# Values kept in DRAM and loaded pair by pair, with a longer ring of weight tiles and another slot order, in a fused attention and gated-MLP kernel

## The chip, the cores and the metric

The kernel runs on one core of one Trainium2 chip. The metric is the device time of one execution in microseconds, taken as the median of three runs.

## The reference, cut to what matters

```python
xn = _layernorm(x, axis=-1)                      # x: 2048 x 512, float32
return x + _A_ref(xn, A_wqkv, A_wo) + _B_ref(xn, B_w_in, B_w_sp, B_b_sp, B_w_out)

# A: 32 heads of 16 columns
q, k, v = qkv[0], qkv[1], qkv[2]
scores = jnp.einsum("bhqd,bhkd->bhqk", q, k) * (Dh ** -0.5)
p = _softmax(scores, axis=-1)
o = jnp.einsum("bhqk,bhkd->bhqd", p, v)
return (lambda x, *d: x.transpose(*d))(o, 0, 2, 1, 3).reshape(B, S, D) @ wo

# B: F = 1792, Fh = 896
z = _gelu(jnp.einsum("bsd,df->bsf", x, w_in))
z1 = z[..., :Fh]
z2 = _layernorm(z[..., Fh:], axis=-1)
g = jnp.einsum("ts,bsf->btf", w_sp, z2) + b_sp[None, :, None]
return jnp.einsum("bsf,fd->bsd", z1 * g, w_out)
```

## The kernel before

**The attention.** The 32 heads run as 16 pairs. For one pair and 512 query columns (a quarter), 16 key tiles of 128 rows are passed. For each key tile TensorE makes the scores of both heads (`scores`, L1232, two matmuls at L1245 into one of three PSUM buffers `sl`), ScalarE takes the exponential into a tile `pf` (`exp`, L1223; `PF` = 8 such tiles), and TensorE multiplies it with V (`values`, L1336, matmuls at L1352). The result of 8 key tiles is added up by `part_out` (L1365). The whole V, with a column of ones behind the 16 columns of each head so that the row sums come out of the same matmul, stays in SBUF as one tile, `vall` (L107); `vpack` (L1010) picks the columns of one head from it, and `v_out` (L422) evicts each 128 rows of V into it with one copy.

**The maxima.** The largest score of each row is needed before the exponential. TensorE makes the scores a second time in the other orientation, one pair ahead (`maxima`, L1251, matmuls at L1259), VectorE reduces 128x1024 of them at a time (`max_red`, L840), and after each 16 such slots `max_fin` (L845 to L860) transposes the maxima, stores them in DRAM (`mscr`) and loads them back as two more rows of the stacked q (`qst`). This is called the exchange here; there are 64. The next scores need its result.

**The dense work.** Everything else that TensorE does is cut into slots of two or four matmuls that a queue of generators hands out: q, k and v, the two halves of the MLP's input product (z2, then z1), the spatial product with w_sp, its output product, and the attention's output product (`attn_out`, L931). One slot is taken by `dense_slot` (L1304, matmuls at L1310) and its results go to PSUM buffers named `dps`. Weights arrive as float32 in a raw tile and are split by POOL into a high and a low part in a second tile (`weight`, L276). Both tiles come from one ring of `RING` = 19 tiles of 128x2x512 (`piece`, L232), in which a raw tile uses one half of its room.

**The order of the work.** TensorE's order is fixed when the program is built, by a planner that keeps a clock of its own for each engine (the `while` loop under `last_turn`). It walks through two strings in turn:

```python
ORDER = ('SMDDSDDMDSDDMDDSDMDDSDMDDSDMDDSDMDDSDDMDMV', 'SMDDDDSDMDDSDMDDSDMDDSDMDDDSDMDDSDDDDMSV')
```

S is a score slot, M a maxima slot, D a dense slot, and V multiplies the 8 P tiles of the string with V. One string up to and with its V is called a cycle here; there are 137, and each holds 8 S, 9 or 7 M in turn, and 24 D. Where no dense slot is ready at the planner's clock (its weights have not been split by then, or the buffers `dps` are not free), a filler stands (`filler`, L1319, matmuls of zeros at L1324). Near the end of the program, when no maxima are left, the planner takes scores and products with V singly. The first cycles are preceded by a written-out opening (`STEPS`, class `First`), which makes the first quarter of q, k, v and the first maxima.

**The end.** The last pair's sums go through `last_pair` (L960), `last_norm` (L974, L976), `last_mm` (L984) and `last_add` (L998, L1003); the dense part of the attention output of two row tiles is added by VectorE at L935 into the tile `fin` that the last add completes. Loads and most stores are issued on SP (`move` and `later`, L142), in the order in which the planner emits them; some stores go out on POOL.

## Time and profile before

| what | value |
|---|---|
| time, median of 3 runs | 1834.79 us (1834.34 to 1835.03) |
| profiled execution, span from first to last instruction | 1830.4 us |
| TensorE (PE) busy | 1800.6 us, 98% of the span, 14742 matmuls |
| VectorE (DVE) busy | 1443.2 us, 79% |
| ScalarE (ACT) busy | 1211.4 us, 66% |
| GpSimd (POOL) busy | 684.5 us, 37% |
| mean granted TensorE clock | 0.999 of full speed |
| DMA engines, hardware queue | 53.3% of the span of 16 engines |

The span is that of one profiled execution; its own time as the runs count it is not given apart from the span, so the 4.4 us between span and median are taken together. A busy share is an average over the whole program. PE counts as busy from a matmul's start to its modelled end, so 98% says that something almost always ran there, not what it was worth.

### The profile page before, as it was taken

The numbers are of one execution on the slowest core, as the hardware profiler recorded it, in microseconds if no ns is written. First come the engines' busy times: TensorE is split into PE (matmuls) and PEld (weight loads), VectorE is DVE, ScalarE is ACT, GpSimd is POOL, SyncE is SP. The second block draws the span as 40 slices with busy tenths as digits, with TensorE's granted clock in tenths as the row PEclk, the third lists the DMA queues.
The fourth block names the chain that finished last, engine by engine and source line by source line (L and its number), as shares of the span: only waits on it lengthen the run. The fifth ranks groups of instructions, "written<-read, shape, count | busy, mean of one in ns | idle before, by whom it ended". The sixth has DMA issues, their size and how long they took to land.

```text
span 1830.4 us, 38100 instructions
## 1 busy us (share of the span) xinstructions
PE 1800.6 (98%) x14742; PEld 1087.6 (59%) x14742; DVE 1443.2 (79%) x1696; ACT 1211.4 (66%) x1329; POOL 684.5 (37%) x786
## 2 busy tenths in 40 slices
PE   9999999999999999999999999999999999999998
PEld 6666566666556565565656655656566665656543
DVE  8857787888888787787877887778778877888882
ACT  4257777888877777666666665666666665666655
POOL 5452241777767776212532244103422140002201
PEclk9999999999999999999999999999999999999999
DMA  7876654433664237647757568655757477466423
GB/s 265 280 240 227 201 190 128 123 114 114 180 190 132 95 105 209 163 137 186 227 144 204 159 188 201 166 143 158 190 146 181 141 210 170 121 156 168 136 88 104
DMA packets 214910, 305.64 MB, mean 167 GB/s; under 512 B 37744, under 2 KB 107952, under 8 KB 214720
## 3 DMA queue, kind: packets, MB, share of 16 engines
q1 hardware_dynamic: 207240, 275.93, 53.3%
q0 software_dynamic: 7488, 27.27, 4.3%
q8 instruction: 116, 1.90, 0.4%
q14 instruction: 66, 0.54, 0.1%
HBM read 193.27 MB, written 109.85 MB: 166 GB/s over the span
## 4 chain that ended last, share of the span: by engine, by line
PE 89%; DVE 5%; DMA 3%; issue 1%; SPq 1%; ACT 1%; POOL 0%; DVEq 0%; ACTq 0%; POOLq 0%
PE dps L1310 35%; PE sl L1352 24%; PE sl L1245 14%; PE sl L1259 12%; DVE mm L840 4%; PE dps L1324 1%; SPq L142 1%; DMA wsp_14r<-in_w_spT 1%; DMA zs<-z2scr 1%; DMA mscr<-ms 0%; PE sl L984 0%; DMA x<-in_x 0%; ACT pf L86 0%; DMA qst<-mscr 0%; DMA qst<-qscr 0%
## 5 line engine op out<-in xcount | busy, mean ns | idle before, releaser
L840 DVE TENSOR_REDUCE mm<-sl 128x2 f32<-128x1024 f32 x1008 | 1208.3, 1222 | 186.0 <-PE sl L1259 177.4
L86 ACT ACTIVATE pf<-sl 128x1024 f32<-128x1024 f32 x1024 | 1043.1, 1026 | 326.7 <-PE sl L1245 288.6
L1352 PE MATMUL sl<-pf,vall 128*32 128x512 f32 x4096 | 467.9, 595 | 0.6 <-DVE on L974 0.6
L1245 PE MATMUL sl<-qst,kst 50*128 50x512 f32 x2048 | 434.6, 417 | 7.7 <-DVE mm L840 2.2
L1259 PE MATMUL sl<-kst,qst 48*128 48x512 f32 x2016 | 414.9, 404 | 3.9 <-DVE mm L840 2.6
L1310 PE MATMUL dps<-wsp,zs 64*128 64x512 f32 x2352 | 381.6, 392 | 0.9 <-DMA zs<-z2scr 0.6
L1245 PEld LDWEIGHTS sl<-qst,kst 50*128 50x128 f32 x2048 | 194.4, 184 | 220.3 <-issue 81.6
L1352 PEld LDWEIGHTS sl<-pf,vall 128*32 128x32 f32 x4096 | 119.2, 109 | 266.5 <-issue 234.9
L1259 PEld LDWEIGHTS sl<-kst,qst 48*128 48x128 f32 x2016 | 191.8, 185 | 104.2 <-ACT pf L86 49.5
L1310 PEld LDWEIGHTS dps<-wsp,zs 64*128 64x128 f32 x2352 | 228.7, 187 | 36.8 <-DMA zs<-z2scr 1.2
L86 ACT ACTIVATE e<-sl 128x512 f32<-128x512 f32 x64 | 38.3, 598 | 189.9 <-PE sl L1352 177.8
L1374 DVE TENSOR_TENSOR e<-sl,e 128x512 f32<-128x512 f32 x64 | 44.2, 691 | 130.2 <-PE sl L1352 80.5
L743 POOL TENSOR_TENSOR hhl<-z1i,hhl 128x512 fp32r<-128x512 f32 x28 | 35.9, 1292 | 280.6 <-ACT hhl L86 280.6
L1310 PE MATMUL dps<-w,xt 64*128 64x448 f32 x768 | 110.5, 368 | 1.7
L1310 PE MATMUL dps<-wout,hp 64*128 64x512 f32 x672 | 110.5, 393 | 0.1
L891 POOL TENSOR_TENSOR ob<-ob 128x512 f32<-128x512 f32 (+1 forms) x16 | 20.6, 1287 | 173.0 <-DMA ob<-rscr 173.0
L1310 PEld LDWEIGHTS dps<-w,xt 64*128 64x128 f32 x768 | 73.7, 186 | 16.1 <-issue 8.4
L1310 PEld LDWEIGHTS dps<-wout,hp 64*128 64x128 f32 x672 | 64.2, 187 | 10.4 <-issue 0.6
L397 POOL TENSOR_TENSOR qkhl<-qr,qkhl 128x512 fp32r<-128x512 f32 x24 | 30.3, 1280 | 97.3 <-ACT qkhl L86 83.0
L887 POOL TENSOR_TENSOR ob<-ob 128x512 f32<-128x512 f32 (+1 forms) x16 | 20.6, 1287 | 99.3 <-DMA ob<-escr 99.3
L1310 PE MATMUL dps<-wf,zs 64*128 64x512 f32 x336 | 55.5, 392 | 0.1
L1310 PE MATMUL dps<-xnT,wqk 64*128 64x512 f32 x288 | 47.9, 394 | 0.3
(298 smaller groups left out, 1692.4 us busy)
## 6 DMA issues: line engine op xcount, KB each, us to landing
zs<-z2scr SPq DMA_DIRECT2D x192, 256.0 KB
escr<-e SPq DMA_DIRECT2D x60, 256.0 KB
hscr<-hhl POOLq DMA_DIRECT2D x28, 512.0 KB, 5.9
qst<-qscr SPq DMA_DIRECT2D x60, 192.0 KB
kst<-kscr SPq DMA_DIRECT2D x60, 192.0 KB
qscr<-qkhl SPq DMA_DIRECT2D x16, 512.0 KB
kscr<-qkhl SPq DMA_DIRECT2D x16, 512.0 KB
xt<-xscr SPq DMA_DIRECT2D x64, 128.0 KB
```

Of the source, the lines that this page charges most:

```text
L86: return nc.scalar.activation(out, in_, func, **kw)
L142: nc.sync.dma_start(raw(dst), raw(src))
L397: nc.gpsimd.tensor_sub(hl[:, 1, :], raw_, hl[:, 0, :].bitcast(F32))
L743: nc.gpsimd.tensor_sub(hl[:, 1, :], z1, hl[:, 0, :].bitcast(F32))
L840: nc.vector.tensor_reduce(mmax[g][:, :, t, kc], sl[k], AX.X, ALU.max)
L887: nc.gpsimd.tensor_add(both_[rows, 0, :], both_[rows, 0, :], both_[rows, 1, :])
L891: nc.gpsimd.tensor_mul(both_[rows, 0, :], both_[rows, 0, :], both_[rows, 1, :])
L1245: nc.tensor.matmul(sl[k][:, j, :], kst[p % 2][rows, kt * P:(kt + 1) * P], qst[p % 2][rows, c * 512:(c + 1) * 512], start=True, stop=True)
L1259: nc.tensor.matmul(sl[k][:, j, :], qst[p % 2][rows, tt * P:(tt + 1) * P], kst[p % 2][rows, kc * 512:(kc + 1) * 512], start=True, stop=True)
L1310: nc.tensor.matmul(bank_of(bank)[:, :w], lhs, rhs, start=go, stop=stop)
L1352: nc.tensor.matmul(sl[k][cols:cols + VW, 0, :], vpack(kt + r, 2 * p + j), pf[:, j * 512:(j + 1) * 512], start=n % CYC == 0, stop=n % CYC = ...
L1374: nc.vector.tensor_add(e, sl[k][:, 0, :], e)
```

## The change

V no longer stays in SBUF. Each 128 rows of V are evicted into a stage tile that is taken from the ring of P tiles (`pf`, now 10 instead of 8), with ones in every 17th column, and stored from there to a new DRAM tensor `vscr`; the 32 columns of pair 0 are also copied straight to their place. Two tiles `vpair` hold the columns of the pair in use and of the next one; `load_v` loads a pair's columns with four DMAs, queued when the pair before has passed its first 8 key tiles (40 for the first). While V is still being made, `exp` leaves two of the ten P tiles to the stages. The ring of weight tiles grows from 19 to 24 tiles, and two raw weight tiles share one tile of it, half each. Both strings of the slot order are new, with the same counts of S, M and D.

```diff
-RING = 19
+RING = 24
-ORDER = ('SMDDSDDMDSDDMDDSDMDDSDMDDSDMDDSDMDDSDDMDMV', 'SMDDDDSDMDDSDMDDSDMDDSDMDDDSDMDDSDDDDMSV')
-PF = 8
+ORDER = ('SMDDSDDMDSDDMDDSMDDDSDMDSDDMDDSDMDDSDDDMMV', 'SMDDDDSDMDSMDSDDDMDDSDMDDDSDMDDSMDDDDDSV')
+PF = 10
...
-    vall = cp.tile([P, NT * H * (DH + 1) + DH - 1], F32, name="vall")
+    vpair = [cp.tile([P, 2 * NT * (DH + 1) + DH - 1], F32, name=f"vpair{a}") for a in range(2)]
...
+    vscr = dr.tile([P, NT, H * (DH + 1)], F32, name="vscr")
...
+    def raw_half(nm):
+        if shared:
+            pair, rest = shared.pop()
+            return pair[:, 1, :], rest
+        pair, rest = piece(nm).bitcast(F32), [2]
+        shared.append((pair, rest))
+        return pair[:, 0, :], rest
...
-        rw = begin(*a)
+        rw, rest = raw_half(nm + "r")
...
-        lease("big", 1)
+        rest[0] -= 1
+        if not rest[0]:
+            lease("big", 1)
...
+    def v_stage(t):
+        vs = at_.tile([P, H * (DH + 1)], F32, tag="pf", name=f"vs{t}", bufs=PF).rearrange("p (h d) -> p h d", d=DH + 1)
+        nc.gpsimd.memset(vs[:, :, DH:], 1.0)
+        return vs
+    def v_take(t, src, copy):
+        copy(vhead(0, t), src[:, 0:2 * DH].rearrange("p (h d) -> p h d", d=DH))
+        vs = staged.pop(t)
+        copy(vs[:, :, :DH], src.rearrange("p (h d) -> p h d", d=DH))
+        return vscr[:, t, :], vs.rearrange("p h d -> p (h d)")
...
     def v_out(t, bank, k):
...
+        while not pfq:
+            yield "C", lambda: pfq
+        gps(0.4)
+        start = pfq.pop(0)
+        staged[t] = v_stage(t)
...
+        store(*pair)
+        pfq.append(ends[0] + 3.0)
...
+    def vpack(p, t, j):
+        i = (2 * t + j) * (DH + 1)
+        return vpair[p % 2][:, i:i + VW]
+    def load_v(p):
+        for i in range(4):
+            w = 2 * (DH + 1)
+            dst = vpair[p % 2][:, 4 * i * w:4 * (i + 1) * w].rearrange("p (t x) -> p t x", x=w)
+            later(0.5 * i, move, dst, vscr[:, 4 * i:4 * i + 4, w * p:w * (p + 1)])
...
-            while not pfq:
-                yield "C", lambda: pfq
+            while not pfq or len(pfq) < 3 and len(vdone) < NT - EARLY:
+                yield "C", lambda: len(pfq) > (0 if len(vdone) == NT - EARLY else 2)
...
+            if vloaded[0] <= p and p + 1 < NP and n_pv >= 64 * p + (40 if p == 0 else 8):
+                vloaded[0] = p + 1
+                load_v(p + 1)
```

TensorE, start of the 31st cycle, where z1 begins, before the change. L1352 is the product with V that closes the cycle ahead, L1245 a score slot, L1259 a maxima slot, L1324 a filler.

```order
L1352 MATMUL sl_202<-pf_5787,vall 32x512 x2
L1245 MATMUL sl_201<-qst_91,kst_93 128x512 x2
L1259 MATMUL sl_203<-kst_92,qst_90 128x512 x2
L1324 MATMUL dps<-brow,zeror 128x512 x2
L1245 MATMUL sl_202<-qst_91,kst_93 128x512 x2
L1324 MATMUL dps<-brow,zeror 128x512 x4
```

The same place in the changed program (product with V L1401, scores L1294, maxima L1308, dense slots L1359):

```order
L1401 MATMUL sl_204<-pf_5861,vpair_88 32x512 x2
L1294 MATMUL sl_203<-qst_92,kst_94 128x512 x2
L1308 MATMUL sl_205<-kst_93,qst_91 128x512 x2
L1359 MATMUL dps<-xnT_0__5734,wf_0_5500 128x512
L1359 MATMUL dps<-xnT_0__5734,wf_0_5523 128x512
...
L1294 MATMUL sl_204<-qst_92,kst_94 128x512 x2
```

Dense slots of z1 stand where the fillers stood. The listings show such fillers inside the cycles of before at the 31st, 32nd, 47th and 48th, around the 62nd, 76th, 90th and 104th and in the last ones; in the changed program every cycle from the third to the last few has its 24 dense slots but the 36th (none, and no fillers) and the 48th (12 fillers instead).

SP, the end of the opening, before: `qst` and `kst` are the stacked q and k, `xscr` the store of the normalized x, `wqk` raw weights, `mscr` the exchange of the maxima.

```order
L142 DMA kst_92<-kscr_98 48x512
L142 DMA xscr_0_102<-xnT_0_349 128x1024
L142 DMA xscr_1_103<-xnT_1_326 128x1024
L142 DMA xscr_2_104<-xnT_2_343 128x1024
L142 DMA xscr_3_105<-xnT_3_353 128x1024
L142 DMA wqk_0r<-in_wqkv 128x4x128
L142 DMA wqk_1r<-in_wqkv 128x4x128
L142 DMA wqk_0r<-in_wqkv 128x4x128
L142 DMA mscr_163<-ms_794 128x32
...
L142 DMA qst_90<-mscr_163 2x16x32 x2
```

And in the changed program:

```order
L142 DMA vscr<-vs_693 128x544
L142 DMA vscr<-vs_717 128x544
L142 DMA qst_91<-qscr_95 48x512
...
L142 DMA vscr<-vs_751 128x544
L142 DMA vscr<-vs_776 128x544
L142 DMA xscr_0_103<-xnT_0_351 128x1024
...
L142 DMA wqk_0r<-in_wqkv 128x4x128 x3
L142 DMA mscr_165<-ms_811 128x32
L142 DMA wqk_0r<-in_wqkv 128x4x128
L142 DMA qst_91<-mscr_165 2x16x32 x2
```

Four stores of V have come in, two of them ahead of the last loads of q and k and two ahead of the stores of x. Further on, the loads of `load_v` (three or four of a pair's four) stand between the store and the reload of the maxima in 15 of the 64 exchanges.

TensorE, in the last cycles, before; L1310 is a dense slot of the attention's output product.

```order
L1245 MATMUL sl_202<-qst_91,kst_93 128x512 x2
L1310 MATMUL dps<-wo_18433,op_0_19789 128x512 x2
L1245 MATMUL sl_203<-qst_91,kst_93 128x512 x2
L1310 MATMUL dps<-wo_18449,op_0_19789 128x512 x6
L1310 MATMUL dps<-wo_18463,ohl_3_19478 128x512 x2
L1245 MATMUL sl_202<-qst_91,kst_93 128x512 x2
L1352 MATMUL sl_201<-pf_19972,vall 32x512 x2
```

And in the changed program:

```order
L1294 MATMUL sl_204<-qst_92,kst_94 128x512 x2
L1373 MATMUL dps<-brow,zeror 128x512 x2
L1294 MATMUL sl_205<-qst_92,kst_94 128x512 x2
L1373 MATMUL dps<-brow,zeror 128x512 x6
L1294 MATMUL sl_204<-qst_92,kst_94 128x512 x2
L1401 MATMUL sl_203<-pf_20038,vpair_88 32x512 x2
```

The dense slots of the last rows have moved ahead of this place, and fillers (L1373) stand there.

## Rows read from the trace of the kernel before

**Rows 1.** View of the core, and part 1 of the page (busy us, share, instructions).

```profile
core 0: 1830.4 us, clock 0.999
...
PE 1800.6 (98%) x14742; PEld 1087.6 (59%) x14742; DVE 1443.2 (79%) x1696; ACT 1211.4 (66%) x1329; POOL 684.5 (37%) x786
```

**Rows 2.** What PE waited for: summed us, count, longest us.

```profile
PE sl L1259 <- DVE mm L840: 2.6, 11, 0.3
PE sl L1245 <- DVE mm L840: 2.2, 8, 0.6
PE dps L1310 <- DVE vall L426: 1.4, 2, 0.9
PE dps L1310 <- DMA zs<-z2scr: 0.6, 1, 0.6
...
PE sl L1245 <- DMA qst<-mscr: 0.2, 1, 0.2
```

**Rows 3.** Timeline of PE, products with V: start us, us, engine, line, operation.

```profile
498.86 3.64 PE L1352 MATMUL sl<-pf,vall 128*32 128x512 f32 x32
...
527.89 3.64 PE L1352 MATMUL sl<-pf,vall 128*32 128x512 f32 x32
...
541.69 3.64 PE L1352 MATMUL sl<-pf,vall 128*32 128x512 f32 x32
...
554.96 1.49 PE L1352 MATMUL sl<-pf,vall 128*32 128x512 f32 x12
...
717.76 3.64 PE L1352 MATMUL sl<-pf,vall 128*32 128x512 f32 x32
...
758.61 3.64 PE L1352 MATMUL sl<-pf,vall 128*32 128x512 f32 x32
...
771.54 3.64 PE L1352 MATMUL sl<-pf,vall 128*32 128x512 f32 x32
...
785.22 1.07 PE L1352 MATMUL sl<-pf,vall 128*32 128x512 f32 x8
...
904.61 3.64 PE L1352 MATMUL sl<-pf,vall 128*32 128x512 f32 x32
...
918.71 3.64 PE L1352 MATMUL sl<-pf,vall 128*32 128x512 f32 x32
...
1698.80 3.64 PE L1352 MATMUL sl<-pf,vall 128*32 128x512 f32 x32
```

**Rows 4.** Groups by line and form: busy us, mean ns of one, idle before.

```profile
L840 DVE TENSOR_REDUCE mm<-sl 128x2 f32<-128x1024 f32 x1008 | 1208.3, 1222 | 186.0 <-PE sl L1259 177.4 <-ACT pf L86 5.3 <-PE sl L1245 1.0
...
L1324 PE MATMUL dps<-brow,zeror 64*128 64x512 f32 x148 | 28.5, 407 | 1.6 <-ACT z1x L86 0.7 <-DVE fin L935 0.6
...
L857 DVE STREAM_TRANSPOSE ms<-mrow 128x32 f32<-128x32 f32 x64 | 13.5, 212 | 2.2
```

**Rows 5.** Timeline of the opening: ScalarE, SP's issues, TensorE's first scores.

```profile
54.78 2.91 SPq L142 DMA_DIRECT2D xscr<-xnT  x4
...
60.82 0.60 ACT L86 ACTIVATE vall<-sl 128x512 f32<-128x512 f32 x1 [4.56 <-PE sl L249]
...
65.78 1.40 SPq L142 DMA_DIRECT2D qst<-mscr  x2
...
74.47 0.40 PE L1245 MATMUL sl<-qst,kst 50*128 50x512 f32 x2
```

**Rows 6.** The chain of waits that ended last: its two longest transfers.

```profile
1406.17 8.06 DMA mscr<-ms
1414.24 5.95 DMA qst<-mscr
```

**Rows 7.** Timeline of VectorE, the tail.

```profile
1820.23 0.29 DVE L976 TENSOR_TENSOR on<-sl,on 128x128 f32<-128x128 f32 x1
...
1823.64 1.22 DVE L935 TENSOR_TENSOR fin<-dps,fin 128x1024 f32<-128x1024 f32 x1
1824.96 1.29 DVE L1003 TENSOR_TENSOR fin<-sl,fin 128x512 f32<-128x512 f32 x2
```

More of the change, by code (lines that the diff above doesn't have):

```diff
@@ L104, in fused_block @@
     nc.gpsimd.memset(brow.bitcast(F32), 0.0)
-    vall = cp.tile([P, NT * H * (DH + 1) + DH - 1], F32, name="vall")
-    vhead = vall[:, :NT * H * (DH + 1)].rearrange("p (t h d) -> p t h d", h=H, d=DH + 1)
+    vpair = [cp.tile([P, 2 * NT * (DH + 1) + DH - 1], F32, name=f"vpair{a}") for a in range(2)]
     mrow = cp.tile([P, 32], F32R, name="mrow")
@@ L274, in bulk @@
         road[0] = max(road[0], clock()) + us
+    shared = []
+    def raw_half(nm):
[5 more added lines that the diff above has]
+        return pair[:, 0, :], rest
     def weight(out, k, a, spare):
@@ L279, in weight @@
         raws[0] += 1
-        rw = begin(*a)
-        n = rw.shape[1]
+        nm, src, n, *blocks = a
+        rw, rest = raw_half(nm + "r")
+        rw = rw[:, :n]
+        if blocks:
+            move(rw.rearrange("p (c f) -> p c f", c=blocks[0]), src.rearrange("(c p) f -> p c f", p=P))
+        else:
+            move(rw, src)
         yield "T", LOAD
         yield open_("big")
-        t = piece(a[0])
+        t = piece(nm)
         yield "G", 0.61
@@ L420, in fused_block @@
     vdone = {}
-    def v_out(t, bank, k):
-        src = (dps if k is None else sl[k])[:, bank, :].rearrange("p (h d) -> p h d", d=DH)
+    def v_stage(t):
[7 more added lines that the diff above has]
+        return vscr[:, t, :], vs.rearrange("p h d -> p (h d)")
+    staged = {}
+    def v_out(t, bank, k):
+        src = (dps if k is None else sl[k])[:, bank, :]
+        while not pfq:
[3 more added lines that the diff above has]
+        staged[t] = v_stage(t)
         if bank:
-            yield "D", td(512)
-            nc.vector.tensor_copy(vhead[:, t, :, :DH], src)
-        else:
-            yield "A", ta(512)
-            act(vhead[:, t, :, :DH], src, AF.Copy)
+            yield "D", td(512) + 0.2, start
+            pair = v_take(t, src, nc.vector.tensor_copy)
+        else:
+            yield "A", ta(512) + 0.23, start
+            pair = v_take(t, src, lambda o, i: act(o, i, AF.Copy))
         if k is None:
@@ L813, in fused_block @@
     stacks = [0]
+    vloaded = [0]
     calm = [True]
@@ L1008, in last_add, with vhead @@
             after(0.1, move, out[(t + a) * P:(t + a + 1) * P, :], fin[t][:, a, :])
-    def vpack(t, h):
-        i = (t * H + h) * (DH + 1)
-        return vall[:, i:i + VW]
+    def vhead(p, t):
+        i = 2 * t * (DH + 1)
+        return vpair[p % 2][:, i:i + 2 * (DH + 1)].rearrange("p (h d) -> p h d", d=DH + 1)[:, :, :DH]
+    def vpack(p, t, j):
[6 more added lines that the diff above has]
+            later(0.5 * i, move, dst, vscr[:, 4 * i:4 * i + 4, w * p:w * (p + 1)])
     def run(gen):
@@ L1125, in ve @@
         def ve(self, t, other):
-            act(vhead[:, t, :, :DH], self.acc["v", t][:, 0, :].rearrange("p (h d) -> p h d", d=DH), AF.Copy)
+            staged[t] = v_stage(t)
+            move(*v_take(t, self.acc["v", t][:, 0, :], lambda o, i: act(o, i, AF.Copy)))
         def m(self, kc, t, other):
@@ L1155, in fused_block @@
             nc.vector.tensor_copy(onesr[r:r + 2, :], ones[0:2, 0:P])
-        nc.gpsimd.memset(vhead[:, :, :, DH:], 1.0)
-        nc.gpsimd.memset(vall[:, NT * H * (DH + 1):], 0.0)
+        for v in vpair:
+            nc.gpsimd.memset(v, 1.0)
         wv = [(qst, kst)[c // 2][1].rearrange("p (b a f) -> p b a f", b=2, a=2)[:, c % 2] for c in range(ND)]
@@ L1351, in values @@
                         cols = VW * (2 * j + r)
-                        nc.tensor.matmul(sl[k][cols:cols + VW, 0, :], vpack(kt + r, 2 * p + j), pf[:, j * 512:(j + 1) * 512], start=n % CYC == 0, stop=n % CYC == CYC - 2)
+                        nc.tensor.matmul(sl[k][cols:cols + VW, 0, :], vpack(p, kt + r, j), pf[:, j * 512:(j + 1) * 512], start=n % CYC == 0, stop=n % CYC == CYC - 2)
                 T["P"] += ROUND
```

## The prediction

> **What bounds the kernel now.** I read the page's first part and the view of the core, then the list of what TensorE (PE in the rows) waited for, then the timeline of the P·V runs, and the timelines of the opening and the tail for what the change adds there. The core view and the first part say that TensorE is busy for 1800.6 of 1830.4 us at a mean granted clock of 0.999 [rows 1]. What is left is therefore the number of slots on its queue, and how evenly they are filled. Its own list of waits is short: 2.6 and 2.2 us for VectorE to hand back a PSUM buffer, 1.4 us for a V eviction, 0.6 us for a load of z2, 0.2 us for one exchange of maxima [rows 2]. No engine behind TensorE holds it up for long.
>
> The loss is not idle time; it stands in the order. A run of 32 P·V matmuls (3.64 us in the timeline [rows 3]) closes one cycle of 8 score slots, 9 or 7 maxima slots in turn, and 24 dense slots. The starts of these runs give the price of a full cycle [rows 3]: 541.69 - 527.89 = 13.80 us with nine maxima and 554.96 - 541.69 = 13.27 us with seven while z1 is computed; 785.22 - 771.54 = 13.68 and 771.54 - 758.61 = 12.93 us from the spatial product on. The listing of before has cycles in which the dense work had run dry (the first listing on the change shows one). They hold fillers (matmuls of zeros) instead, hardly get shorter, and their dense slots come later as extra work. In the changed order these holes are gone, except two.
>
> **The change, step by step.** The sum is made on the profiled span, 1830.4 us; the median of the runs is 1834.79 us, 4.4 us more, which lies around the span and which I take as unchanged.
>
> 1. Dense supply (ring of 24, halved raw weights; the slot order moves with it). In the stretch from 498.86 to 717.76 [rows 3] stand 16 cycles, 218.90 us. Sixteen full ones are 8 x 13.80 + 8 x 13.27 = 216.6. The changed listing has 15 full ones and one (the 36th) with no dense slot at all and no fillers: 8 scores and 7 maxima that alternate on three PSUM buffers. Seven reductions of 1222 ns [rows 4] are 8.6 us, with the P·V run of 3.64 and about 0.7 of turns 12.9 us, 0.4 less than a full one. So 216.2, a gain of 2.7.
> From 717.76 to 1698.80 [rows 3] stand 73 cycles, 981.04 us: 37 x 13.68 + 36 x 12.93 = 971.6. Four cycles, at the first unit of each spatial group, wait by plan in both listings (904.61 to 918.71 = 14.10, so 0.4 each): 973.3. One cycle (the 48th) has twelve fillers and no dense slot; I leave it at 12.9. The gain is 7.7. Of this I give 0.6 back, the wait for a z2 load [rows 2], since nothing in the change moves it. Step 1: -9.8. Lower end: nothing, if the operands of the dense slots come late on the chip (below); upper end -12, if the two holes are as cheap as 12 us each.
> Eleven filler slots fewer are part of this; a filler matmul shows 407 ns of busy time [rows 4], but in the nine-maxima cycles one stands where TensorE would wait anyhow, so I price cycles, not fillers.
>
> 2. The slot order itself. In the full cycles a few maxima move by one to five slots, the counts stay. All waits of TensorE that such a shift can take away are 2.6 + 2.2 us [rows 2], so the gain ends at -4.8. On the other side a maxima or score slot now comes up to one slot earlier after the one whose buffer it takes; 0.1 us in each of some 45 pairs of full cycles would be +4.5. I take 0, in the middle.
>
> 3. The opening. Sixteen V tiles are now evicted by two copies: a full one (0.60 us on ScalarE [rows 5], as before) and one of 32 columns for pair 0. The nearest small VectorE operation is the transpose of 128x32 at 212 ns [rows 4]; with 0.1 for the turn I take 0.3 each. Fourteen are covered by other work; two evictions already hold TensorE for 1.4 us together [rows 2], so +0.6. If the cover goes everywhere, 12 x 0.3 = +3.6.
> The stores of V queue on SP. The second listing on the change shows the last two ahead of four stores of xnT and three weight loads; they wait for the eviction of tile 2, which ends at 60.82 + 0.60 [rows 5], while the xnT stores ran at 54.78 before. From about 62.3 us the four stores take 2.91 us [rows 5] and the weight loads about as long, so the store and reload of the first maxima come some 5 us later: the reload at 70.8 instead of 65.78 [rows 5], done issuing at 72.2. The first scores stood at 74.47 [rows 5] and need it landed. That leaves 2.3 us for the landing; I put the wait at +1.0, between 0 and +3. The two V stores ahead of the load of the last K columns add 0.4. Step 3: +2.0, from 0 to +5.
>
> 4. V in DRAM. Fifteen pairs are loaded by four DMAs each, one pair ahead, seven cycles before use (three for the second pair), so some 40 us at the least and no P·V run waits for them. What they pass is the exchange of the maxima: in 15 of 64 exchanges three or four of these loads now stand on SP between the store of the maxima and their reload. An issue costs about 0.73 us where four xnT stores take 2.91 [rows 5], so up to 2.9 us each. Before, one exchange used up its whole time: the store landed after 8.06 us, the reload after 5.95 [rows 6], and TensorE waited 0.2 [rows 2]. I take +0.6, from 0 to +3.
>
> 5. The tail. In before the dense slots of the last two row tiles stand between the last scores, the last P·V runs and the output matmuls; the third listing shows fillers there instead, and the dense sum of those rows is added earlier. After the last multiplication on VectorE (1820.23 + 0.29) the output needs two rounds on TensorE and VectorE, but ends only at 1824.96 + 1.29 [rows 7], with the add of the dense sum, 1.22 us, in between [rows 7]. Without that add and the dense slots I get -2.0, and three fewer slots before it give -0.7 (bounded by 3 x 0.8 of filler pairs [rows 4]). Step 5: -2.7, from -1 to -4.
>
> Sum: -9.8 + 0 + 2.0 + 0.6 - 2.7 = -9.9. Span 1820.5, time 1834.8 - 9.9 = **1824.9 us**, with its own range 1818 to 1831. Ten P buffers instead of eight add nothing of their own: every run of 8 tiles still follows its own 8 scores in the listing, and the two extra buffers serve the V tiles.
>
> **The rivals.**
> (a) The supply stands in the order but not on the chip: the plan lets weights be split and z2 loaded earlier, and the queues are not that fast, so TensorE stops at the dense slots where it ran fillers before. For it: the slots are placed by the plan's own clock. Against it: in before TensorE waited 0.6 us in all for such loads [rows 2]. Step 1 would shrink to about -2; the rest is -0.1, so 1832.7. 13%.
> (b) The clock falls in the 36th cycle, where TensorE has 15 slots in some 9 us and nothing between them. No stretch of before is so thin, and the clock stood at 0.999 [rows 1]. If the level of 1.2 GHz were granted, the next run of 3.64 us [rows 3] would take as long again, and the slots behind it some 2 us: +6, 1831. 7%. The Trainium skill (TensorE: Matmul & The Clock Gate, Part 1) has the clock gated down until activity releases it, and down again after idleness, which speaks against a cycle without fillers; no row of before shows which way it goes here, and by the page's reading the sum would be 1831 instead of 1825.
> (c) Slower: the V loads turn the exchange of maxima into the bound. Scores of every four row tiles wait for it on TensorE's queue, so dense slots behind them wait too. It decides once the 15 exchanges are late by (9.9 + 3.7) / 15 = 0.9 us each on the average. If half of the up to 2.9 us of issues reached TensorE in each, 15 x 1.45 = 22 us, less 9.9: 1847. For it: the exchange that took 14 us [rows 6]. Against it: only one of 64 waited. 8%. The Trainium skill (DMA: Bandwidth & Descriptors, Specifications) puts the smallest transfer at line rate at 512 bytes; the pieces of these loads are 34 x 4 = 136 bytes, so by the page they run below it and this rival gains. The row nearest to that is the store of the maxima, 32 x 4 = 128 bytes a piece, and where it shows it took 8.06 us [rows 6], which agrees.
> (d) The earlier maxima free VectorE and all 4.8 us of step 2 come on top: 1820. 10%.
>
> **How the numbers follow.** The forecast keeps 62%. 0.2% of this kernel, about what a measurement can tell from no change, is 3.7 us: faster means below 1831.1, slower above 1838.5. Faster: 60 of the 62, all of (d), 4 of (b), 2 of (a): 76%. Slower: (c) and 1 of (a): 9%. Same: the remaining 15%. The range 1816 to 1834 reaches from the upper ends of steps 1, 2 and 5 to rival (a) and leaves out (c) and some of each end.
>
> **What would show it.** P·V runs at even steps of 13.3 to 13.9 and 12.9 us through the z1 and spatial stretch, without the longer ones between; one step of about 12.9 without fillers; scores of the first pair a microsecond late; the add of the last dense sum no longer between the last output adds. It is wrong if waits for weights or z2 appear at the dense slots, if waits of the scores for the reload of maxima pass 5 us, or if the steps of the full cycles change by more than 0.1 us.

## The result and the profile after

The changed kernel takes **1841.13 us** (median of five runs, 1839.61 to 1843.12) against 1834.79 for the kernel before beside it: a ratio of 1.0034, 95% interval 1.0022 to 1.0047. It is slower where a gain of 9.9 us was forecast. In a second set of runs the ratio was 1.0049 (1.0034 to 1.0064). The profiled execution took 1839.61 us, its span is 1837.3, and its mean granted clock 0.996 where before had 0.999 [rows 1].

Part 1 of the page of after: TensorE is busy for 4.6 us less than before, and the span is 6.9 us longer.

```profile
span 1837.3 us, 38176 instructions
...
PE 1796.0 (98%) x14720; PEld 1089.5 (59%) x14720; DVE 1444.6 (79%) x1702; ACT 1207.7 (66%) x1339; POOL 684.6 (37%) x802
```

What TensorE waited for in after (sum in us, count, longest); L1308 are maxima, L1294 scores, L1401 the products with V:

```profile
PE sl L1308 <- ACT pf L86: 4.5, 6, 2.5
PE sl L1308 <- DVE mm L878: 3.6, 13, 0.6
PE sl L1294 <- DVE mm L878: 3.1, 11, 0.7
PE sl L1401 <- DVE vpair L445: 2.7, 1, 2.7
PE sl L1294 <- DMA qst<-mscr: 2.6, 2, 1.6
```

Against [rows 2] two waits are new, for a V eviction in front of a product with V (2.7 us) and for the reload of the maxima in the opening (2.6; the 0.2 of before stood later in the program). The wait of the maxima for ScalarE's exponentials has grown from 1.0 to 4.5 us, and the two waits for VectorE's reductions from 4.8 to 6.7. None is a wait of a dense slot for its weights.

Timeline of PE in after, products with V (the same stretches as [rows 3]):

```profile
119.40 3.62 PE L1401 MATMUL sl<-pf,vpair 128*32 128x512 f32 x26
125.67 1.06 PE L1401 MATMUL sl<-pf,vpair 128*32 128x512 f32 x6 [2.66 <-DVE vpair L445]
...
136.90 1.49 PE L1401 MATMUL sl<-pf,vpair 128*32 128x512 f32 x12
...
507.12 1.06 PE L1401 MATMUL sl<-pf,vpair 128*32 128x512 f32 x8
...
575.32 3.64 PE L1401 MATMUL sl<-pf,vpair 128*32 128x512 f32 x32
...
588.83 5.32 PE L1401 MATMUL sl<-pf,vpair 128*32 128x512 f32 x32
...
604.57 1.92 PE L1401 MATMUL sl<-pf,vpair 128*32 128x512 f32 x16
...
726.50 1.07 PE L1401 MATMUL sl<-pf,vpair 128*32 128x512 f32 x8
...
1707.14 1.06 PE L1401 MATMUL sl<-pf,vpair 128*32 128x512 f32 x8
```

Cut at these starts, the two spans compare as follows (us; the sums are the spans). Cycles are numbered by the product with V that ends them; each profile holds 128 such products, so there are 128 cycles, not 137.

| stretch | before | forecast | after |
|---|---|---|---|
| start to the 1st product with V | 87.95 | with the 2nd: +2.0 | 92.13 |
| 2nd cycle | 27.07 | | 27.27 |
| 3rd cycle | 13.89 | as before | 17.51 |
| 4th to 30th | 369.95 | as before | 370.22 |
| 31st to 46th (z1) | 218.90 | 216.2 | 219.38 |
| 47th to 119th (spatial product on) | 981.04 | 973.3, +0.6 given back | 980.64 |
| the rest | 131.60 | 128.9 | 130.16 |

The holes of before (places where dense slots are missing and fillers stand) are gone as the listing said: the 31st and 32nd cycles take 27.3 instead of 29.0 us, the 76th to 78th 39.5 instead of 42.4. But the z1 and spatial stretches together are as long as before, so as much was lost elsewhere in them. Four places lose time, two of them in these stretches.

**The 36th cycle.** Windows of TensorE in after (busy us, matmuls, granted clock, DMA share, GB/s):

```profile
575.00:580.00 5.00, 4.63 (x40) 1.00 0.05 8
580.00:585.00 5.00, 4.08 (x16) 0.70 0.15 54
585.00:590.00 5.00, 4.70 (x20) 0.50 0.14 52
590.00:595.00 5.00, 5.00 (x34) 0.77 0.47 132
```

Busy time does not show it (4.70 of 5.00 us), the count of matmuls and the clock do: in the cycle without dense slots or fillers the granted clock falls to the lower of its two levels (0.50, that is 1.2 GHz), and the product with V behind it takes 5.32 us instead of 3.64. The 36th and 37th cycles take 13.51 and 15.74 us, where 12.9 and 13.80 were counted on: 2.5 us.

**The lone sum.** The spatial product takes its column tiles in twos; the last of each group stands alone, is made in two halves, and GpSimd adds these up (L770). Timeline of GpSimd, ScalarE and TensorE in the 61st cycle of after: this sum starts at 917.96, behind weight splits (L303); ScalarE's next instruction needs it and waits 5.52 us, with exponentials queued behind, and TensorE waits 2.52 us for those.

```profile
906.45 1.29 POOL L929 TENSOR_TENSOR ob<-ob 128x512 f32<-128x512 f32 x1 [2.52 <-DMA ob<-rscr]
...
916.70 1.29 POOL L303 TENSOR_TENSOR wsp<-wsp_7r,wsp 128x512 fp32r<-128x512 f32 x1
917.96 1.25 POOL L770 TENSOR_TENSOR z1i<-z1i,z1b 128x512 f32<-128x512 f32 x1
...
919.25 0.63 ACT L86 ACTIVATE hhl<-z1i 128x512 fp32r<-128x512 f32 x1 [5.52 <-POOL z1i L770]
...
920.84 0.51 PE L1308 MATMUL sl<-kst,qst 48*128 48x512 f32 x2 [2.52 <-ACT pf L86]
```

The same sum in the kernel before, where GpSimd was idle and waited for VectorE:

```profile
906.81 1.27 POOL L733 TENSOR_TENSOR z1i<-z1i,z1b 128x512 f32<-128x512 f32 x1 [1.65 <-DVE z1i L730]
```

In all three cycles two or three weight tiles more are split ahead of the sum than before, and GpSimd has no idle time left there. In the 61st it had also stood 2.52 us for a load of the attention's output (`ob`, L929 above), with the splits behind it.

The 61st, 75th and 89th cycles take 16.71, 14.65 and 15.41 us, where I had 14.1 for each: 4.5 us.

**The 3rd cycle.** Timeline of ScalarE and VectorE in after: the evictions of V into stage tiles wait for earlier stores of V to land, VectorE's follow ScalarE's, and the product with V at 125.67 (above) waits for the last.

```profile
118.50 0.60 ACT L86 ACTIVATE vs<-sl 128x512 f32<-128x512 f32 x1 [4.62 <-DMA vscr<-vs]
...
124.80 0.60 ACT L86 ACTIVATE vs<-dps 128x512 f32<-128x512 f32 x1 [5.08 <-DMA vscr<-vs]
...
125.43 0.19 DVE L445 COPY vpair<-dps 128x32 f32<-128x32 f32 x1 [5.50 <-ACT vs L86]
```

**The opening.** SP's issues in after, from the second of two V stores on:

```profile
62.07 0.34 SPq L142 DMA_DIRECT2D vscr<-vs  x1
62.45 3.25 SPq L142 DMA_DIRECT2D xscr<-xnT  x4
...
69.25 0.46 SPq L142 DMA_DIRECT2D mscr<-ms  x1
...
73.11 1.39 SPq L142 DMA_DIRECT2D qst<-mscr  x2
```

SP had stood up to 5.1 us for a V eviction on ScalarE ahead of these. The reload of the maxima is issued at 73.11 us instead of 65.78 [rows 5]; the first scores wait for it twice, 2.6 us together.

### The profile page after: what moved, and what is told of

Its sections match the earlier page's. It is cut to its first block, busy times and chain, and to the rows that moved or that the text cites. A ratio compares the mean times of both kernels' runs of the same rounds, so it can differ in the third digit from the quotient of the medians.

```text
span 1837.3 us, 38176 instructions
## 1 busy us (share of the span) xinstructions
PE 1796.0 (98%) x14720; PEld 1089.5 (59%) x14720; DVE 1444.6 (79%) x1702; ACT 1207.7 (66%) x1339; POOL 684.6 (37%) x802
## 3 DMA queue, kind: packets, MB, share of 16 engines
q0 software_dynamic: 7488, 27.27, 4.7%
## 4 chain that ended last, share of the span: by engine, by line
PE 89%; DVE 4%; DMA 2%; issue 1%; POOL 1%; ACT 1%; SPq 1%; DVEq 0%; ACTq 0%; POOLq 0%
PE dps L1359 35%; PE sl L1401 24%; PE sl L1294 14%; PE sl L1308 12%; DVE mm L878 4%; PE dps L1373 1%; SPq L142 1%; ACT pf L86 1%; DMA vscr<-vs 1%; DMA w_2r<-in_w_in 1%; PE sl L247 1%; PE sl L248 0%; PE sl L249 0%; PE sl L1022 0%; POOL w L303 0%
## 5 line engine op out<-in xcount | busy, mean ns | idle before, releaser
L1401 PE MATMUL sl<-pf,vpair 128*32 128x512 f32 x4096 | 470.6, 597 | 3.3 <-DVE vpair L445 2.7
L1294 PE MATMUL sl<-qst,kst 50*128 50x512 f32 x2048 | 435.2, 418 | 11.5 <-DVE mm L878 3.1
L1308 PE MATMUL sl<-kst,qst 48*128 48x512 f32 x2016 | 412.0, 404 | 8.3 <-ACT pf L86 4.5
L1359 PE MATMUL dps<-wsp,zs 64*128 64x512 f32 x2352 | 373.5, 392 | 0.0
L1294 PEld LDWEIGHTS sl<-qst,kst 50*128 50x128 f32 x2048 | 194.8, 184 | 221.8 <-DVE mm L878 92.1
L1401 PEld LDWEIGHTS sl<-pf,vpair 128*32 128x32 f32 x4096 | 119.5, 110 | 271.2 <-issue 236.1
L1308 PEld LDWEIGHTS sl<-kst,qst 48*128 48x128 f32 x2016 | 191.8, 185 | 107.0 <-ACT pf L86 51.3
L1359 PEld LDWEIGHTS dps<-wsp,zs 64*128 64x128 f32 x2352 | 226.8, 187 | 35.0
L1359 PE MATMUL dps<-w,xt 64*128 64x448 f32 x768 | 110.3, 368 | 1.8
L1359 PE MATMUL dps<-wout,hp 64*128 64x512 f32 x672 | 107.2, 393 | 0.0
L929 POOL TENSOR_TENSOR ob<-ob 128x512 f32<-128x512 f32 (+1 forms) x16 | 20.5, 1281 | 171.5 <-DMA ob<-rscr 137.5
L1359 PEld LDWEIGHTS dps<-w,xt 64*128 64x128 f32 x768 | 73.5, 186 | 16.3 <-issue 8.6
L1359 PEld LDWEIGHTS dps<-wout,hp 64*128 64x128 f32 x672 | 64.7, 187 | 9.7
L1359 PE MATMUL dps<-wf,zs 64*128 64x512 f32 x336 | 54.0, 393 | 0.0
L1359 PE MATMUL dps<-xnT,wqk 64*128 64x512 f32 x288 | 47.1, 394 | 0.2
```

What stands on the lines that cost most here:

```text
L929: nc.gpsimd.tensor_mul(both_[rows, 0, :], both_[rows, 0, :], both_[rows, 1, :])
L1294: nc.tensor.matmul(sl[k][:, j, :], kst[p % 2][rows, kt * P:(kt + 1) * P], qst[p % 2][rows, c * 512:(c + 1) * 512], start=True, stop=True)
L1308: nc.tensor.matmul(sl[k][:, j, :], qst[p % 2][rows, tt * P:(tt + 1) * P], kst[p % 2][rows, kc * 512:(kc + 1) * 512], start=True, stop=True)
L1359: nc.tensor.matmul(bank_of(bank)[:, :w], lhs, rhs, start=go, stop=stop)
L1401: nc.tensor.matmul(sl[k][cols:cols + VW, 0, :], vpack(p, kt + r, j), pf[:, j * 512:(j + 1) * 512], start=n % CYC == 0, stop=n % CYC == CYC ...
```

## Experiments

"Ratio" is to the kernel before, whose runs stood beside each group (22 to 28 a group); below 1 is faster. Times of different groups are compared by their ratios.

### One place at a time

**Repeated matmuls in the 36th cycle**

```diff
 def scores():
-            for j in range(2):
+            for j in (0, 1) * (2 if n_pv == 8 * 35 else 1):
 def maxima():
-            for j in range(2):
+            for j in (0, 1) * (3 if n_pv == 8 * 35 else 1):
```

> The changed kernel, in whose 36th cycle (no dense slots, no fillers) each score matmul is issued twice and each maxima matmul three times with the same operands; nothing else differs. Theory: TensorE's granted clock falls to the lower level because it has little to do there; kept busy, it keeps the clock, the run of P.V matmuls behind it takes 3.64 us again instead of 5.32, the 36th and 37th cycles together 26.7 to 27.1 us instead of 29.25, the granted clock of the whole run is above 0.998, and the time falls by 2.5 to 5 us from 1841.1. Rival: the clock falls for a reason elsewhere (the dense work pausing, or nothing that the order sets); then P.V stays at 5.3 us and the time stays within 1 us or rises by the added matmuls.

Measured: 1839.25 us, ratio 1.0026 (1.0015 to 1.0036). The clock is 1.00 in all windows from 575 to 600 us, and the product with V is back:

```profile
591.21 3.64 PE L1401 MATMUL sl<-pf,vpair 128*32 128x512 f32 x32
```

So the clock falls because the cycle is thin. But the repeats lengthen the 36th cycle to 14.90 us; both cycles take 28.92, only 0.3 less. Half of the expectation held: by the ratios the time falls by 1.5 us against the first set of the changed kernel and by 4 against the second, with run clocks of 0.995 to 0.997, not above 0.998.

**Two more places for V**

```diff
+        if t == 12:
+            vs = vpair[1][:, :w]
+        elif t == 13:
+            vs = at_.tile([P, w], F32, tag="vs", name="vs13", bufs=1)
...
-        ms = at_.tile([P, 32], F32, tag="ms", name=f"ms{g}", bufs=2)
+        ms = at_.tile([P, 32], F32, tag="ms", name=f"ms{g}", bufs=1)
```

> The changed kernel with two more places for V on its way to DRAM: tiles 12 and 13 are staged in the idle second pair tile and in a tile of their own instead of P tiles (the transposed maxima have one tile instead of two for it). The order on every engine is the same. Theory: the product with V of the 3rd cycle waits because the last V evictions wait until the stores of the V tiles before them have landed and given their P tile back; with two more places ScalarE's waits of 4.6 and 5.1 us for these stores go, the 3rd cycle takes 13.9 us instead of 17.5, and the time falls by 3.0 to 3.8 us. Rival: the evictions are late because everything on the DMA queues is late there (weights, stores of prepared weights); then the wait moves to another operand and less than 1 us is gained.

Measured: 1842.88 us, ratio 1.0043 (1.0029 to 1.0057). In the profile the 3rd cycle takes 13.80 us and the evictions wait for no store, so the cause of that wait is shown. The time does not show it: the profiled execution took 1837.60 us at a clock of 0.996, the other five 1840.03 to 1844.95 at 0.992 to 0.994. So the expected fall of the time by 3 us and more is not shown. This kernel still has the stall of the opening (its first product with V starts at 93.83 us); the run of the unchanged kernel, below, shows what that can do. The other five executions have no profile.

**The lone sum on VectorE**

```diff
-        nc.gpsimd.tensor_add(z1, z1, z1b)
+        nc.vector.tensor_add(z1, z1, z1b)
```

> The changed kernel with one instruction on another engine: the sum of the two halves of the lone spatial product (four in all) is made by VectorE instead of GpSimd. TensorE's, ScalarE's and SP's orders are the same. Theory: in the 61st, 75th and 89th cycles this sum stands on GpSimd behind weight splits that the larger ring lets in earlier, ScalarE's queue waits for it (5.5 us at most), and TensorE's scores and maxima wait for ScalarE; without GpSimd in that chain these cycles take 13.7 to 14.1 us instead of 16.71, 14.65 and 15.41, and the time falls by 4 to 5.5 us. Rival: the exponentials are late there for another reason, or the sum on VectorE delays the reductions as much; then less than 1 us is gained.

Measured: 1838.83 us, ratio 1.0029 (1.0020 to 1.0037); 13.89, 14.11 and 14.10 us for the three cycles, 4.7 less than in after. That the sum's place on GpSimd's queue is the cause is shown; the edit does not tell the splits from the wait for `ob` in the 61st. Of the size the time gives back between 1 and 4 us, as one takes the first or the second set of the changed kernel.

**The opening's V stores on GpSimd's queue**

```diff
-            move(*v_take(t, self.acc["v", t][:, 0, :], lambda o, i: act(o, i, AF.Copy)))
+            nc.gpsimd.dma_start(*v_take(t, self.acc["v", t][:, 0, :], lambda o, i: act(o, i, AF.Copy)))
```

> The changed kernel, in whose opening the four stores of V tiles are issued on GpSimd's queue instead of SP's; nothing else differs. Theory: on SP they hold up the stores and loads behind them, so the first reload of the maxima comes late and the first scores wait 2.6 us for it; off SP these waits go, the first product with V starts 2.5 to 3.5 us earlier than 92.1 us, and the time falls by 2 to 3.5 us. Rival: the first scores are late because the DMA queues are fuller (more bytes in the opening), or GpSimd, now waiting for the evictions, is late with q and k; then the start moves by less than 1 us, or later.

Measured: 1835.63 us, ratio 1.0011 (1.0002 to 1.0020). The wait for the reload is gone, and the first product with V starts at 87.2 us, before that of the kernel before. This is the largest single effect: 4 us against the first set of the changed kernel, 7 against the second, by the ratios, more than the wait itself and more than I expected. The next run shows a reason.

**The changed kernel again**

> The changed kernel, nothing edited, on the chip and beside the runs of the other three. All theories: ratio to the kernel before 1.0034 within 0.001, a granted clock of 0.992 to 0.996 over the run. What its profile adds: the theory of local stalls has the wait for the first reload of the maxima (2.6 us in the first profile, 2.8 to 3.2 us in three of the runs that kept it) and the fall of the clock behind it at 75 to 85 us come and go between executions, so that the first product with V starts at 92 to 95 us; a rival that puts the time into the order alone has both profiles alike within 1 us in every cycle.

Measured: 1843.72 us, ratio 1.0049 (1.0034 to 1.0064), clocks of 0.991 to 0.995; I had 1.0034 within 0.001. Its profile is of an execution of 1846.66 us. Windows of TensorE in it:

```profile
55.00:60.00 5.00, 3.97 (x15) 0.83 0.32 101
60.00:65.00 5.00, 4.53 (x22) 0.83 0.17 64
...
75.00:80.00 5.00, 2.08 (x13) 0.88 0.85 268
80.00:85.00 5.00, 4.96 (x24) 0.50 1.07 342
85.00:90.00 5.00, 3.60 (x23) 0.84 1.04 404
90.00:95.00 5.00, 4.89 (x34) 0.76 1.04 401
...
925.00:930.00 5.00, 3.36 (x16) 0.53 1.04 291
930.00:935.00 5.00, 5.00 (x36) 0.79 0.96 249
```

Windows of the first profile, behind the same waits:

```profile
75.00:80.00 5.00, 2.38 (x15) 1.00 1.03 340
80.00:85.00 5.00, 3.60 (x29) 1.00 1.06 342
```

Behind the waits for the reload (1.32 and 1.56 us here, 1.05 and 1.57 there) the clock falls in this execution and not in the first. The clock had been at 0.83 from 55 to 65 us here too, and the reload is issued at 74.64 instead of 73.11. The first product with V starts at 97.61 instead of 92.13 us, later than the 92 to 95 I expected. The profiles of the three runs above that keep these stores on SP show the fall as well (0.59 to 0.81 in the window from 80 to 85 us, first product with V at 93.83 to 94.99); the one without them has 1.00 there.

In the 61st cycle the wait of TensorE for ScalarE is 3.72 us here, the clock falls behind it, and the cycle takes 20.30 us, 6.2 more than the 14.1 I had; in the first profile the wait was 2.52 us, the clock stayed, and the cycle cost 2.6 more. So in this cycle a stall cost about its own length where the clock stayed, and more where it fell. The rival, both profiles alike within 1 us in every cycle, is out. That this is why the kernel's times spread, and why its median lies above its first profile, fits the runs (of the eleven, the two slowest ran at 0.991 and 0.992, the fastest at 0.995) but only two of them have a profile.

The Trainium skill (TensorE: Matmul & The Clock Gate, Part 1) has the clock gated down after idleness. The windows behind the stalls agree; in the 36th cycle TensorE was thin rather than idle, and the clock fell all the same.

### All four, and what is left

**All four edits together**

> The changed kernel with the edits of the four runs before together: the opening's V stores on GpSimd, two more places for V on its way, the lone sum on VectorE, repeated matmuls in the 36th cycle. Theory: the losses are local and add up: opening -4.5, 3rd cycle -3, 61st, 75th and 89th cycles -4.5, the 36th and 37th -0.5, so 12 to 13 us less than the changed kernel, a ratio to the kernel before of 0.996 to 0.9975: faster than before, which is the supply's gain at last. Rival: what is won in one place is waited for in the next, since the DMA queues or GpSimd bound the whole stretch; then at most half of it shows and the ratio stays above 0.9995.

Measured: 1831.14 us, ratio 0.9984 (0.9975 to 0.9994), clocks of 0.996 to 0.999. Together the four edits give back 9 to 12 us, so the rival is out; the changed kernel with them is faster than before, by somewhat less than I wrote. How much each gives is not measured cleanly, since the single runs kept the opening's stall.

**The hole closed by the planner instead**

```diff
-AGE = 9.0
+AGE = 8.0
```

> As the last, but the hole of the 36th cycle is not filled with repeated matmuls: the planner lets a low-priority step wait for 8 instead of 9 us, so the tanh of z1 goes to ScalarE a little earlier, and by the listing the 36th cycle has its 24 dense slots (three fillers in the 33rd, some in the 47th and 48th instead). Theory: TensorE is never thin, no fall of the clock at 580 to 595 us, and the time is 1.5 to 3 us below that of the kernel with repeated matmuls: a ratio to before of 0.9945 to 0.9965. Rival: the hole was cheap in itself and the clock was not the cost; then both are within 1 us of each other.

Measured: 1833.27 us, ratio 0.9994 (0.9985 to 1.0003). This expectation failed. The hole is gone and the clock is 1.00 there, but the new order has other losses: every second cycle from the 50th to the 102nd, those with seven maxima, takes 13.15 instead of 12.94 us, some 5 us in all; in the profiled execution, the slowest of its eleven, the 61st takes 17.14 and the 115th 18.79 us. The same 0.2 us stands in six cycles of before and eight of after; I did not follow its cause.

**The slot order alone, in the kernel before**

```diff
-ORDER = ('SMDDSDDMDSDDMDDSDMDDSDMDDSDMDDSDMDDSDDMDMV', 'SMDDDDSDMDDSDMDDSDMDDSDMDDDSDMDDSDDDDMSV')
+ORDER = ('SMDDSDDMDSDDMDDSMDDDSDMDSDDMDDSDMDDSDDDMMV', 'SMDDDDSDMDSMDSDDDMDDSDMDDDSDMDDSMDDDDDSV')
```

> The kernel before with both strings of the slot order of the changed one and nothing else; by the listing its holes are those of before within a few fillers. Theory: where a slot stands in a full cycle is worth nothing here, since full cycles took the same in both profiles (13.80 and 13.27, 13.68 and 12.95 us): ratio 0.9995 to 1.0005. Rival: the order has a part in the loss, its maxima come too close to each other: ratio 1.001 to 1.003, with more waits of scores and maxima for VectorE than 4.8 us.

Measured: 1830.56 us, ratio 0.9981 (0.9972 to 0.9989): 3.5 us faster by the ratio. The full cycles are what they were, and TensorE's waits for VectorE are 5.4 us (4.8 before), so neither theory is right. What changes in the profile is where the holes fall: the 47th to 49th cycles take 39.7 instead of 40.9 us, the 104th to 107th 53.8 instead of 54.9, and the trace has 138 filler matmuls (L1324) instead of 148, with 8 in the 48th cycle instead of 16. No run tests this reading by itself.

**V in DRAM, the ring and the halves with the old slot order and three edits** (the diff above the other way, and the second, third and fourth edit)

> The changed kernel with both strings of the slot order of before, and with the edits for the opening's V stores, the two more places for V and the lone sum; no repeated matmuls, since by the listing the 36th cycle has its 24 dense slots then (holes only in the 47th, 4 fillers, and the 117th to 119th). It leaves of the change the V in DRAM, the ring of 24 and the halved raw tiles. Theory: the supply of dense slots is worth much of what I priced (9.8 us) once the local stalls are out, with the old order too: a ratio to before of 0.995 to 0.998. Rival: the gain of the kernel with four edits is that of the slot order, which alone gave 0.9981 in the kernel before, and the supply is worth nothing: 0.9995 to 1.0005.

Measured: 1837.97 us, ratio 1.0020 (1.0011 to 1.0029): slower than before. The rival's value was 1.000; it is worse. Its profile has holes and waits of its own (the 47th to 50th cycles take 57.3 us against 53.8, the 60th 15.79 against 12.96, and the clock falls to 0.50 at 1700 us, in the hole of the 119th). With the old order the earlier supply shows no gain; which part of this kernel loses the time is not taken apart.

**Half the repeats**

```diff
 def scores():
-            for j in (0, 1) * (2 if n_pv == 8 * 35 else 1):
+            for j in (0, 1) * (1 if n_pv == 8 * 35 else 1):
 def maxima():
-            for j in (0, 1) * (3 if n_pv == 8 * 35 else 1):
+            for j in (0, 1) * (2 if n_pv == 8 * 35 else 1):
```

> The kernel with four edits, with half the repeats in its 36th cycle: maxima matmuls twice, score matmuls once. Theory: that still keeps the clock, and the cycle is set by its reductions again: 36th and 37th cycles together 27.0 to 27.4 us instead of 28.94, no fall of the clock at 575 to 595 us, ratio about 0.9975. Rival: it is too little for the clock, which falls as in the changed kernel: product with V 5 us and more, both cycles 29 us, ratio 0.9985 to 0.9995.

Measured: 1829.35 us, ratio 0.9972 (0.9963 to 0.9981). The ratio is the theory's, the profile is the rival's: the clock falls at 575 to 585 us in it (0.70, 0.61), and both cycles take 29.4 us. That execution took 1831.26 us at a clock of 0.997; four others ran at 0.999 and 1.000 and took 1826.92 to 1829.50, but two at 0.996 took 1828.82 and 1829.20. Whether the clock holds in the 36th cycle of the faster ones is not seen: one profile does not tell.

What still holds TensorE up in it, beside VectorE: late weight splits, at dense slots in the 62nd and 76th cycles (14.98 and 14.20 us).

```profile
PE dps L1366 <- POOL wsp L303: 2.0, 2, 1.3
```

**The slot order and the lone sum, V in SBUF** (the diff of the order and that of the lone sum, in the kernel before)

> The kernel before with the slot order of the changed one and the lone sum on VectorE: the candidate that keeps V in SBUF. Theory: ScalarE's waits for GpSimd at the lone sum (7.1 us in three in the profile of before, its cycles 14.10, 14.13 and 14.08 us) are a small part of the same stall, so the 61st and 75th cycles take 13.7 us: 0.5 to 1 us below the order alone, ratio 0.9975 to 0.998. Rival: they were hidden there: 0.998 to 0.9985.

Measured: 1830.15 us, ratio 0.9976 (0.9962 to 0.9989). The 61st and 75th cycles stay at 14.09 and 14.12: the sum was no part of the loss there. This kernel and the one with half the repeats (0.9972) beat both kernels of the study, and can't be told from each other.

**The 36th cycle left empty, the three other edits made**

> The changed kernel with the three edits that take local stalls away (opening's V stores on GpSimd, two more places for V, lone sum on VectorE) and the 36th cycle left as it is, empty of dense slots and fillers. Theory: only the hole is left of the four losses: the clock falls at 575 to 595 us, 36th and 37th cycles 29.2 us, ratio to before 0.998 to 0.9995, some 2 us above the kernel with repeats (0.9972). Rival: the hole costs nothing that the repeats gave back; then it lies at 0.997 to 0.9975.

Measured: 1831.63 us, ratio 0.9992 (0.9983 to 1.0000); the product with V takes 5.27 us, both cycles 28.8. The theory's value: 3 to 4 us above the kernel with half the repeats, by the ratios. The two profiles do not show where, since the clock falls in both of them (0.67 and 0.65 here from 575 to 585 us), and against the kernel with all repeats (0.9984) the intervals overlap. So what the hole costs over many executions is not settled.

**The kernel before without the fillers of its 31st and 32nd cycles**

```diff
-            for r, bank in zip((0, 64), (halves if begun else (0, 1))):
+            for r, bank in zip((0, 64), (halves if begun else (0, 1))) if n_pv // 8 not in (30, 31) else ():
```

> The kernel before without the seventeen filler slots of its 31st and 32nd cycles (matmuls of zeros; 114 filler matmuls are left of 148); everything else stands where it stood. Theory: a stretch that is thin costs clock in any of the kernels: granted clock at 0.5 to 0.8 between 500 and 530 us, a product with V of 5 us there, the 31st to 33rd cycles together 44.5 to 48 us instead of 42.8, ratio 1.001 to 1.002. Rival: the fillers do nothing, TensorE only waits in their place: the clock stays, ratio 0.9995 to 1.0005.

Measured: 1838.01 us, ratio 1.0028 (1.0019 to 1.0037): 34 matmuls of zeros fewer cost 4.7 us. Windows of TensorE in it, and the product with V of the 32nd cycle's end:

```profile
500.00:505.00 5.00, 4.27 (x32) 1.00 0.43 129
505.00:510.00 5.00, 4.49 (x16) 0.50 1.01 397
510.00:515.00 5.00, 5.00 (x28) 0.50 1.04 308
515.00:520.00 5.00, 5.00 (x44) 0.97 0.29 81
```

```profile
530.50 6.22 PE L1352 MATMUL sl<-pf,vall 128*32 128x512 f32 x32
```

In the kernel before the clock stands in the same stretch:

```profile
505.00:510.00 5.00, 4.88 (x34) 1.00 0.97 376
510.00:515.00 5.00, 5.00 (x48) 1.00 0.98 314
```

The 31st to 33rd cycles take 48.8 us instead of 42.8. The rival is out: the fillers hold the clock, and a hole without them costs time in either kernel, 6.0 us in this profile and 2.5 in that of after.

### The loads of V

**Each pair's V loaded twice** (`load_v(p + 1)` called a second time)

> The kernel with four edits, in which each pair's V columns are loaded twice: 60 more loads on SP, twice as many between the store of the maxima and their reload. Theory: the loads cost nothing where they stand, since scores wait for no reload after the opening: ratio to before 0.998 to 0.999, as without them, and no wait of scores for the reload in the profile after 140 us. Rival (my slower case): the exchange is near its limit, so that doubled issues of up to 2.9 us each bring waits of scores for the reload of 5 us and more, and a ratio 0.003 to 0.01 higher.

Measured: 1935.92 us, ratio 1.0554. Scores wait for the reload in each of the 15 exchanges:

```profile
PE sl L1301 <- DMA qst<-mscr: 79.7, 15, 9.7
```

SP's queue in one of them:

```profile
228.43 11.74 SPq L142 DMA_DIRECT2D vpair<-vscr x6
...
240.77 1.26 SPq L142 DMA_DIRECT2D qst<-mscr  x2
```

The second load of a tile has to wait for the first, and SP stands meanwhile (150.2 us in 60 waits). So this shows what a wait on SP in front of the reload costs, 7 us a pair, and not what the loads cost; it was the wrong experiment for that question.

**The same loads in eight pieces**

```diff
-        for i in range(4):
+        for i in range(8):
```

(with two key tiles a piece instead of four, `later(0.25 * i, ...)`)

> The kernel with four edits and half the repeats, in which a pair's V columns are loaded by eight DMAs of two key tiles instead of four DMAs of four: the same bytes and pieces, twice the issues on SP, none of which waits for another. Theory: scores found the reload landed 4.3 to 8 us after its issue in the exchanges that V loads share, and another 1.5 to 2 us of issues is still covered: ratio as without them, 0.9965 to 0.998, no wait of scores for the reload after 140 us above 1 us in all. Rival (my slower case at its own scale): the exchange has no room left, waits of 1 us and more in most of the 15 exchanges, and a ratio above 1.002.

Measured: 1831.98 us, ratio 0.9987 (0.9979 to 0.9996), and no wait of scores for the reload after 140 us. The wait that would carry my slower case is not there even with twice the issues. The ratio lies above the theory's range and below the rival's; that it is 0.0015 above that of four pieces, with lower clocks (0.994 to 0.998), stays open.

## Why the prediction was wrong

**Step 1, the supply of dense slots, is the step that failed.** It priced cycles by the listing: "15 full ones and one (the 36th) with no dense slot at all and no fillers", at 12.9 us, and "four cycles, at the first unit of each spatial group", at 14.10. The full cycles came as priced, 13.8 and 13.28, 13.67 and 12.95. Both special prices were wrong. The 36th cost 2.5 us more with the one behind it: the sum of its reductions was nearly right (13.51), but it had no term for the clock, and the cycle behind took 15.74. The 61st, 75th and 89th cost 4.5 more: 14.10 was read from the order of before, and in the new one the lone sum came late on GpSimd and TensorE waited for ScalarE; eight late cycles took 0.2 us more each, and a few single waits make up the rest. Instead of 9.8 the two stretches gave nothing (218.90 to 219.38, 981.04 to 980.64). I had read the list of TensorE's waits [rows 2] as a property of the kernel. It is one of the order: weights that are split earlier stand on GpSimd's queue ahead of something else. The three signs of being wrong that I named did not show it: no dense slot waited for weights or z2, the reload cost 2.6 us and not 5, and the full cycles came as priced but for the eight late ones. The time was lost beside them.

**Step 2, the slot order**, was put at 0 between -4.8 and +4.5. In the kernel before it is worth -3.5 us, inside the bounds, and by a way I had not named: full cycles are alike, holes move. In the changed kernel with the same three edits it is worth more: 0.9992 with the new order, 1.0020 with the old. Since the order alone reaches 0.9981, the whole gain of the repaired kernel can be the order's; that V in DRAM and the longer ring give something beside it is not shown.

**Step 3, the opening**: +2.0, "from 0 to +5". The mechanism was right: V stores ahead of the four stores of x, 62.45 us for the first of these where I had 62.3, the reload late. It came at 73.11 instead of 70.8: the store of the maxima was issued 5.9 us later than before (69.25 against 63.36), and the reload followed it after 3.9 us instead of 2.4. The wait was 2.6 instead of 1.0: +4.4 by the second product with V, +9.8 in the second profile, where the clock fell behind the wait. The size of the wait was off by more than a factor of two, and what a wait of TensorE costs behind itself was left out.

**Step 4, V in DRAM**: the loads, priced at +0.6, cost nothing that shows. But "ten P buffers instead of eight add nothing of their own ... the two extra buffers serve the V tiles" passed over the place where they are too few: the last V tiles follow each other faster than their stores land, ScalarE waits 4.6 and 5.1 us for these, and the 3rd cycle pays 3.6 us in the first profile (1.7 to 2.3 in the four other profiles that keep this staging).

**Step 5, the tail**: -2.7, "from -1 to -4"; measured -1.4 (131.60 to 130.16). Right in kind: the add of the dense sum no longer stands between the last adds on VectorE,

```profile
1827.54 0.29 DVE L1014 TENSOR_TENSOR on<-sl,on 128x128 f32<-128x128 f32 x1
...
1830.71 1.28 DVE L1041 TENSOR_TENSOR fin<-sl,fin 128x512 f32<-128x512 f32 x2
```

and the last add ends 4.2 us after the last multiplication instead of 5.7 [rows 7]. But from there the program takes 5.3 us to its end instead of 4.2, for which the prediction has no term; why is open.

**The rivals.** (b), the clock in the 36th cycle, came true at 7%, with 2.5 us of the 6 I gave it in the profiled execution; the median execution may pay more, since the clock can fall at the other stalls too. (a) is half true: supply was not late at the dense slots of after (in the kernel with half the repeats it was, by 2.0 us in two places), its work on GpSimd was late for others. (c), the slower case, was wrong: no exchange behind the opening waited, and the time came out slower for other reasons. (d) did not come: the waits for VectorE grew to 6.7 us.

The sum of what was missed in the first profile: 2.4 in the opening, 3.6 in the 3rd cycle, 2.5 in the 36th and 37th, 4.5 at the lone sums, 1.6 in late cycles, 1.3 in the tail, together 15.9 of the 16.8 us between forecast span (1820.5) and measured (1837.3).

## What to carry to other kernels

In a kernel like this one, whose TensorE is full, a stall can cost more than its length when the clock falls behind it, so count matmuls and clock in a window, not busy time. When a change lets work run ahead, ask on whose queue it will stand, and who waits behind that queue in order; a list of waits from the kernel before does not answer it. Price a new order from where its holes fall, and run the order alone before crediting the buffers that came with it.

## What the runs showed that I had not expected

Matmuls of zeros are worth their place: 34 of them hold 4.7 us. And taking V stores off SP, which ended 2.6 us of waiting for a reload in the opening, gave 4 to 7 us of the whole.
